# A lap in front of TensorE's loop that only branches through its program, in a decode attention kernel

## The chip, the cores and the metric

One core of a Trainium2 chip runs the whole kernel. The metric is device time in microseconds (us) of one execution, as the median of several runs. The core's engines are TensorE (PE in the profile, its weight loads PEld), VectorE (DVE), ScalarE (ACT), GpSimd (POOL) and SyncE (SP); each runs its own program, and they meet at semaphores. Sixteen DMA engines move data between main memory and the core's buffers.

## The reference

Attention for one new token: 32 query heads of 128 numbers, 8 heads of keys and values with 65,536 rows each, so that 4 query heads share one head of keys and values. Everything is bfloat16.

```
B, Hq, Hkv, Sq, Sk, D = 1, 32, 8, 1, 65536, 128
k = jnp.repeat(k, rep, axis=1)
v = jnp.repeat(v, rep, axis=1)
scale = D ** -0.5
scores = jnp.einsum("bhqd,bhkd->bhqk", q, k) * scale
p = _softmax(scores, axis=-1)
return jnp.einsum("bhqk,bhkd->bhqd", p, v)
```

Keys and values together are 268 MB, and each number of them is used for four query heads only.

## The kernel before

The work is cut into 16 pairs of units, two pairs to each of the 8 heads. A unit is 16,384 rows of keys and as many of values, laid out as 128 partitions with 128 rows each; `T` is 128, and the unit is handled in `G` = 16 groups of `TB` = 8 tiles of 128 x 128. A pair has 8.39 MB of keys and 8.39 MB of values.

TensorE's program (`tensor_engine`, L177) first transposes the queries (L180), which need a small DMA, and then runs a loop of 16 laps (`Fori`, L182), one for each pair. Its body, `pe_pair` (L164), is written out in full:

- for both units, group by group, eight transposes of key tiles into one of four PSUM buffers `trb` (`pe_transposes`, L131), and three groups behind (`LAG`) the eight score matmuls of an earlier group (`pe_scores`, L140);
- then for both units 128 matmuls that sum the values, weighted, in `pvb` (`pe_values`, L158). In the last lap only, one more matmul (L151) stands in the second unit's sum behind an `If` (L149).

So a lap has 768 matmuls, each with a weight load, and about 50 semaphore instructions. VectorE and ScalarE copy the transposed groups to the buffer `ktb` (`evict`, L189 to L201: VectorE three of four, ScalarE the fourth), find the maximum (L219), compute the exponentials (L336) and keep the sums.

SyncE issues all large DMAs, in the order keys of pair 0, values of pair 0, keys of pair 1, values of pair 1, and so on (L402 to L435). Pair 0's keys come as four transfers of 2 MB (L396) and its values as two of 4 MB (L428). The keys of pairs 1 to 13 come as one transfer of 8 MB into `kbuf` (L408); its second half is copied to `bbuf` by GpSimd and ScalarE (`copy_unit`, L203). There is one set of buffers for keys and one for values, so two waits order these issues: keys of the next pair wait for `kfree`, which comes when the last group of the first unit has been taken out of `trb` (L197), and for `cfree`; values of the next pair wait for `vfree`, which VectorE gives when the second unit's values have been summed (L284, L296). While TensorE works on keys, the queue holds the values, and the other way round.

ScalarE's part of the copies, two pieces in each of those laps, is made in `act_pair` behind the evictions of the groups 3 and 7. `own` (L118) lets an engine wait for its own instruction, and `copy_unit` calls it for the last of its pieces.

## Time and profile before

| | |
|---|---|
| runs (3) | median 628.36 us, 628.25 to 628.51 |
| the profiled execution | 628.33 us |
| its span, first to last instruction | 627.0 us |
| TensorE's mean granted clock | 0.773 |
| busy: PE, DVE, ACT, POOL | 489.3, 315.3, 231.7, 159.9 us |
| moved | 268.57 MB, mean 428 GB/s |
| packets of queue q8, kind instruction | 6, 0.10 MB |

The profile is of one execution. Its page has the busy share of every engine in 40 slices, the DMA queues, the chain of work that ended last, and groups of instructions; the views of the trace that are quoted below list instructions in order of time, or the waits, or the busy time by stretches. Times in them are microseconds from the first instruction. "Issue" as a releaser means that an engine stood still and the profile shows nothing that it waited for; "PEq" is the sequencer of TensorE, which takes the semaphores.

### The profile page before, as it was taken

The page shows a single profiled execution, that of the slowest core. Times are in us where ns is not written, and L with a number is a line of the kernel's source. Part 1 is how long each engine was busy: PE and PEld are TensorE (multiplying, and loading weights), DVE is VectorE, ACT ScalarE, POOL GpSimd, SP SyncE. Part 2 cuts the span into 40 slices and gives each one's busy share as a digit, 9 for nine tenths or more (in the row PEclk, how much of TensorE's full clock was granted, in tenths as well). Part 3 has the DMA queues.
Part 4 walks back from the last instruction along what each step waited for, and adds up shares of the span by engine and source line. Part 5 has one row for each costly group of instructions (what it writes and reads, how often), then busy time and mean ns, then how long its engine had stood idle before and what let it go on. Part 6 is the DMA issues. An engine that isn't in the chain of part 4 may idle for free. (4 is left out here: it accounts for less than half of the span.)

```text
span 627.0 us, 27922 instructions
## 1 busy us (share of the span) xinstructions
PE 489.3 (78%) x12292; PEld 482.7 (77%) x12292; DVE 315.3 (50%) x699; ACT 231.7 (37%) x445; POOL 159.9 (26%) x124
## 2 busy tenths in 40 slices
PE   4843995949859598694976949779596895999996
PEld 4842995949859598694977949679596895989896
DVE  4630653717537174471744718346183561848482
ACT  1320542515435153341634407244062441624241
POOL 0000704307042070520606115060250702400000
PEclk9875886959769597795977959669596885969696
DMA  8999999999999999999999999999999999999997
GB/s 368 433 454 424 439 431 439 431 439 431 439 422 447 414 452 414 452 414 440 431 426 439 431 439 431 439 431 439 431 439 431 439 431 435 418 429 431 418 431 316
DMA packets 6768, 268.57 MB, mean 428 GB/s; under 512 B 1000, under 2 KB 1128, under 8 KB 1256
## 3 DMA queue, kind: packets, MB, share of 16 engines
q1 hardware_dynamic: 6712, 268.45, 99.3%
q8 instruction: 6, 0.10, 0.1%
q10 hardware_dynamic: 48, 0.01, 0.0%
q14 instruction: 2, 0.02, 0.0%
HBM read 268.44 MB, written 0.01 MB: 428 GB/s over the span
## 5 line engine op out<-in xcount | busy, mean ns | idle before, releaser
L201 DVE COPY ktb<-trb 128x1024 bf16<-128x1024 bf16 x384 | 254.9, 689 | 169.1 <-PE trb L131 165.1
L199 ACT ACTIVATE ktb<-trb 128x1024 bf16<-128x1024 bf16 x128 | 131.0, 1023 | 341.1 <-PE trb L131 287.6
L131 PE MATMUL trb<-ident,kbuf 128*128 128x128 bf16 x2048 | 180.6, 247 | 94.9 <-PEq L46 94.8
L131 PEld LDWEIGHTS trb<-ident,kbuf 128*128 128x128 bf16 x2048 | 146.1, 112 | 95.8 <-issue 95.6
L207 POOL COPY bbuf<-kbuf 128x2048 bf16<-128x2048 bf16 x78 | 143.9, 1893 | 174.8 <-POOLq L46 174.8
L140 PE MATMUL qkb<-qcur,ktb 128*128 128x4 bf16 x4096 | 176.8, 165 | 9.2 <-PEq L46 7.3
L140 PEld LDWEIGHTS qkb<-qcur,ktb 128*128 128x128 bf16 x4096 | 158.2, 97 | 15.3 <-issue 15.0
L131 PE MATMUL trb<-ident,bbuf 128*128 128x128 bf16 x2048 | 156.9, 219 | 3.6 <-issue 3.6
L158 PE MATMUL pvb<-pts,vbuf 128*128 128x4 bf16 x4096 | 113.3, 166 | 23.2 <-PEq L46 12.8
L158 PEld LDWEIGHTS pvb<-pts,vbuf 128*128 128x128 bf16 x4096 | 111.3, 103 | 25.0 <-issue 24.1
L131 PEld LDWEIGHTS trb<-ident,bbuf 128*128 128x128 bf16 x2048 | 117.3, 97 | 1.1 <-issue 1.1
L382 POOL PARTITION_ALL_REDUCE cmaxa<-cmax x32 | 11.9, 370 | 252.3 <-POOLq L46 252.3
L336 ACT ACTIVATE pts<-qkb,negm 128x128 bf16<-128x128 f32 x128 | 50.5, 546 | 0.0
L345 ACT ACTIVATE bbuf<-kbuf 128x2048 bf16<-128x2048 bf16 x26 | 49.5, 1902 | 0.0
L336 ACT ACTIVATION_READ_ACCUMULATOR pts<-qkb,negm 128x1 f32 x128 | 35.4, 277 | 0.0
L219 DVE TENSOR_REDUCE cmax<-qkb 128x4 f32<-128x512 f32 x32 | 22.0, 686 | 19.3 <-DVEq L46 19.3
L332 ACT ACTIVATE alpha<-dm 128x4 f32<-128x4 f32 x32 | 6.4, 201 | 43.5 <-ACTq L46 43.5
L247 DVE TENSOR_TENSOR acc<-acc,pvb 128x4 f32<-128x4 f32 x16 | 2.5, 158 | 34.5 <-PE pvb L158 34.5
L384 POOL PARTITION_ALL_REDUCE la<-lp x8 | 3.4, 430 | 33.1 <-POOLq L46 33.1
L245 DVE COPY acc<-pvb 128x4 f32<-128x4 f32 x8 | 1.3, 163 | 17.8 <-PE pvb L158 17.8
L229 DVE TENSOR_TENSOR m<-m,cmaxa 128x4 f32<-128x4 f32 x24 | 3.9, 164 | 11.7 <-DVEq L46 11.5
L238 DVE TENSOR_TENSOR acc<-acc,alpha 128x4 f32<-128x4 f32 x24 | 3.9, 163 | 11.3 <-DVEq L46 11.3
(42 smaller groups left out, 39.1 us busy)
## 6 DMA issues: line engine op xcount, KB each, us to landing
vbuf<-in_v_dram SPq DMA_DIRECT2D x5, 4096.0 KB, 25.7
kbuf<-in_k_dram SPq DMA_DIRECT2D x4, 2048.0 KB, 15.5
bbuf<-in_k_dram SPq DMA_DIRECT2D x4, 2048.0 KB, 20.2
kbuf<-in_k_dram SPq DMA_DIRECT2D x1, 4096.0 KB, 16.3
bbuf<-in_k_dram SPq DMA_DIRECT2D x1, 4096.0 KB, 16.0
vbuf<-in_v_dram SPq DMA_DIRECT2D x1, 2336.0 KB, 29.0
vbuf<-in_v_dram SPq DMA_DIRECT2D x1, 1216.0 KB, 31.5
vbuf<-in_v_dram SPq DMA_DIRECT2D x1, 416.0 KB, 32.0
```

What stands on the lines that cost most here:

```text
L131: ins = pe.transpose(trb[j % NTB][:, i * P:(i + 1) * P], kv[:, t, :], ident[:, :])
L140: ins = pe.matmul(qkb[n][:, t * R:(t + 1) * R], lhsT=ktb[:, off:off + P], rhs=qcur[:, :], start=True, stop=True)
L158: ins = pe.matmul(pvb[n][:, 0:R], lhsT=vv[:, t, :], rhs=pts[n][:, t * R:(t + 1) * R], start=t == 0, stop=t == T - 1)
L199: e.activation(dst, trb[j % NTB][:, :], AF.Copy).then_inc(eva, 1)
L201: e.tensor_copy(dst, trb[j % NTB][:, :]).then_inc(evd, 1)
L207: ins = op(bbuf[:, c * CB * D:(c + 1) * CB * D], kbuf[:, off:off + CB * D])
L219: e.tensor_reduce(cmax[:, :], qkb[n][:, :].rearrange("p (t g) -> p g t", g=R), AX.X, ALU.max).then_inc(cm, 1)
L229: own(e, e.tensor_tensor(mn[:, :], mo[:, :], cmaxa[:, :], ALU.max), xd)
L332: e.activation(alpha[:, :], dm[:, :], AF.Exp, scale=scale)
L336: ins = e.activation(pv[:, g, :], sv[:, g, :], AF.Exp, bias=negm[:, g:g + 1], scale=scale, accum_out=rsum[:, g:g + 1])
L345: return e.activation(o, i, AF.Copy)
L382: e.partition_all_reduce(cmaxa[:, :], cmax[:, :], P, bass.bass_isa.ReduceOp.max).then_inc(cma, 1)
```

## The change

TensorE's loop has 17 laps in place of 16. The steps of `pe_pair` are first put in a list, with the values cut into steps of eight tiles, which makes 96 steps. The list is cut into sections of 14 steps (252 // 18), seven in all, and each is put behind a branch of its own, `If(lap > 0)`. In the first lap all seven branches are taken past their sections, and nothing else is done. At the end of the body, behind another branch (`If(lap == 0)`), stand the wait for the queries, their transpose and the wait for the float identity, which stood ahead of the loop. The `If` of the last lap compares with `NP` now in place of `NP - 1`. The matmuls, their order and their semaphores are those of before.

In `copy_unit`, an engine that gives no semaphore of its own doesn't wait for its copy; the copy itself raises the semaphore that TensorE waits for. ScalarE's first piece (behind group 3) uses this; the second piece still waits.

```
+SECTION = 252
...
-    def pe_values(pe, n, lap):
+    def pe_values(pe, n, t0, lap):
         vv = vbuf[:, n * T * D:(n + 1) * T * D].rearrange("p (t d) -> p t d", d=D)
-        for t in range(T):
+        for t in range(t0, t0 + TB):
             if n and t == V_PIECES[1][0]:
-                with pe.If(lap == NP - 1):
+                with pe.If(lap == NP):
...
-        ins.then_inc(pvd, 1)
+        if t == T - 1:
+            ins.then_inc(pvd, 1)
 
     def pe_pair(pe, lap):
-        pend = []
+        steps, pend = [], []
         for n in range(2):
             for j in range(G):
-                pe_transposes(pe, n, j)
+                steps.append((pe_transposes, n, j))
                 pend.append((n, j))
                 if len(pend) > LAG:
-                    pe_scores(pe, *pend.pop(0))
-        while pend:
-            pe_scores(pe, *pend.pop(0))
-        for n in range(2):
-            pe_values(pe, n, lap)
+                    steps.append((pe_scores, *pend.pop(0)))
+        steps += [(pe_scores, *x) for x in pend]
+        steps += [(pe_values, n, t, lap) for n in range(2) for t in range(0, T, TB)]
+
+        per = SECTION // (2 * TB + 2)
+        for i in range(0, len(steps), per):
+            with pe.If(lap > 0):
+                for f, *x in steps[i:i + per]:
+                    f(pe, *x)
 
     def tensor_engine(pe):
-        pe.wait_ge(q_sem, 16)
-        pe.wait_ge(t_id, 1)
-        pe.transpose(qps[:, 0:HR], qsb[:, :], ident[0:HR, 0:HR]).then_inc(s_x, 1)
-        pe.wait_ge(t_if, 1)
-        with pe.Fori(0, NP) as lap:
+
+        with pe.Fori(0, NP + 1) as lap:
             pe_pair(pe, lap)
+            with pe.If(lap == 0):
+                pe.wait_ge(q_sem, 16)
+                pe.wait_ge(t_id, 1)
+                pe.transpose(qps[:, 0:HR], qsb[:, :], ident[0:HR, 0:HR]).then_inc(s_x, 1)
+                pe.wait_ge(t_if, 1)
...
-                if c != copies[-1]:
+                if c != copies[-1] or not x:
                     ins.then_inc(done, 1)
-            own(e, ins, x)
-            e.sem_inc(done, 1)
+            if x:
+                own(e, ins, x)
+                e.sem_inc(done, 1)
...
-                copy_unit(e, (lap - (WHOLE[0] - 1)) * (WHOLE[1] - lap) > 0, ACT_COPIES[j], copy, cpa, xa)
+                copy_unit(e, (lap - (WHOLE[0] - 1)) * (WHOLE[1] - lap) > 0, ACT_COPIES[j], copy, cpa, xa if j == max(ACT_COPIES) else None)
```

## The prediction

> **What bounds the kernel now.** I read the page first: the slices, the queues, the chain that ended last.

> ```profile
> DMA  8999999999999999999999999999999999999997
> GB/s 368 433 454 424 439 431 439 431 439 431 439 422 447 414 452 414 452 414 440 431 426 439 431 439 431 439 431 439 431 439 431 439 431 435 418 429 431 418 431 316
> ...
> q1 hardware_dynamic: 6712, 268.45, 99.3%
> q8 instruction: 6, 0.10, 0.1%
> ...
> DMA 5%; PE 1%; SPq 0%; DVE 0%; issue 0%; DVEq 0%
> ...
> L131 PE MATMUL trb<-ident,kbuf 128*128 128x128 bf16 x2048 | 180.6, 247 | 94.9 <-PEq L46 94.8
> ```

> DMA is at 9 tenths in every slice but the first and the last, and the chain that ended last is DMA. The kernel is bound by moving 268.45 MB; no slice in between shows a hole to close. TensorE waits 94.9 us for keys, about 6.3 us in each of 15 laps. So the edit can cost time only by making a transfer start after its queue ran dry, and can gain hardly anything in the middle. Whether a transfer starts late depends on the first lap, so I read stretches of it (busy time by engine, granted clock, DMA share, GB/s) and SyncE's issues.

> ```profile
> 1.00:2.00 1.00, 0.00 (x0) 0.00 (x0) 0.52 (x3) 0.84 (x1) 0.38 (x1) 1.00 0.80 180
> 0.00:40.00 40.00, 27.50 (x582) 26.90 (x583) 20.65 (x53) 11.45 (x20) 1.46 (x8) 0.93 0.96 406
> 43.00:60.00 17.00, 5.51 (x187) 5.28 (x186) 0.81 (x5) 0.00 (x0) 0.00 (x0) 0.50 1.01 435
> ```

> ```profile
> 0.72 0.88 SPq L396 DMA_DIRECT2D kbuf<-in_k_dram  x2
> 1.65 1.14 SPq L396 DMA_DIRECT2D bbuf<-in_k_dram  x2
> 2.97 0.86 SPq L428 DMA_DIRECT2D vbuf<-in_v_dram  x2
> 21.01 0.33 SPq L408 DMA_DIRECT2D kbuf<-in_k_dram  x1
> 55.99 0.33 SPq L431 DMA_DIRECT2D vbuf<-in_v_dram  x1
> ```

> And how long the transfers of L428 (pair 0's values, two) and of L408 (pair 1's keys) took to land, from the queries of these two lines:

> ```profile
> DMA to landing us min/median/max: 30.7/35.4/40.1
> ...
> DMA to landing us min/median/max: 41.8/41.8/41.8
> ```

> Pair 0's keys and values are 16.78 MB. 40 us at 406 GB/s are 16.24 MB, the rest at 435 takes 1.2 us: on the mean the queue would be dry at 41.2 us, on the slowest engine near 43.4 (3.3 + 40.1, the landing). Pair 1's keys were issued at 21.0, far ahead. They are 8.39 MB, 19.3 us: dry again at 60.5 on the mean, and landed at 62.8 (21.0 + 41.8). Pair 1's values were issued at 55.99. From issue to data takes about 0.9 us (issue at 0.72; 0.42 us worth of traffic before 2.0, so a start near 1.6). **The slack is thus 18 to 21 us for pair 1's keys, and 3.6 to 5.9 us for its values.** These two bounds decide the case.

> **What the first lap pays for its program.** Next, TensorE's timeline of that lap.

> ```profile
> 8.29 3.57 PE L131 MATMUL trb<-ident,kbuf 128*128 128x128 bf16 x32 [2.95 <-PEq L46]
> ...
> 14.77 0.61 PE L131 MATMUL trb<-ident,kbuf 128*128 128x128 bf16 x8
> ...
> 20.18 0.21 PE L140 MATMUL qkb<-qcur,ktb 128*128 128x4 bf16 x3 [0.17 <-issue]
> ...
> 27.94 0.26 PE L131 MATMUL trb<-ident,bbuf 128*128 128x128 bf16 x1 [2.61 <-issue]
> ...
> 35.21 0.56 PE L131 MATMUL trb<-ident,bbuf 128*128 128x128 bf16 x7 [0.95 <-issue]
> ...
> 46.41 3.53 PE L158 MATMUL pvb<-pts,vbuf 128*128 128x4 bf16 x127 [6.33 <-issue]
> 53.61 0.28 PE L158 MATMUL pvb<-pts,vbuf 128*128 128x4 bf16 x5 [3.68 <-issue]
> ...
> 62.98 0.37 PE L131 MATMUL trb<-ident,kbuf 128*128 128x128 bf16 x2 [7.21 <-PEq L46]
> ```

> Five stops stand in the midst of a tile, with no releaser ("issue"), and none recurs in later laps. Between the stops at 46.41 and 53.61 lie 127 matmuls: with their weight loads and two semaphore instructions 256 instructions. Six instruction packets make 0.10 MB, 16 KB each; 256 instructions of 64 bytes fill one. So a stop is the arrival of a program block, and after the first lap the loop stays loaded. Stops that add up to 13.7 us (0.17 + 2.61 + 0.95 + 6.33 + 3.68) delay TensorE in lap 0, but the last values of pair 0 still end early enough: 55.99 lies 3.6 us or more ahead of need. **What the edit removes is off the path.**

> [...]

> **The price of the lap in front.** It cannot hide behind tiles, since it has none. Each section is under 256 instructions, so every branch lands in the same block or the next, and blocks are asked for one after another. Counting back 256 instructions from the stop at 20.18 leads to the eighth group's transposes at 14.77: that block was entered there, and the next was usable at 20.18, so 5.4 us from one entry to the next while 2 MB transfers fill the queues. Later ones took 7.8 (20.18 to 27.94), 7.3 (to 35.21), 11.2 (to 46.41) and 7.2 (to 53.61). Two blocks were there at the start (nothing stops before 20.18); the seven sections end in the seventh block, so five arrivals are walked through.

> Engines begin at 0.7 us; the loop's start and a taken branch bring 1.0. Four arrivals fall before 24 us, at 5.4: 22.6. The fifth meets the larger transfers, at 7.4 (between the 7.8 and 7.3 above): **30.0 us for the walk's end.** No row shows an arrival with the queues empty. Were each as quick as a data issue, 0.9 us, the walk would end at 5.5; with five at 7.4 it would end at 38.0. I stay near the five measured arrivals, since the data queues are full from 1.6 us on.

> Lap 1's end is SyncE's next issue of values:

> ```profile
> 95.19 0.33 SPq L431 DMA_DIRECT2D vbuf<-in_v_dram  x1
> ```

> Then come the transpose of the queries, the loop's branch and the wait for keys long landed: 0.5 us, so the first transposes at 30.5 in place of 8.29. The queries need no term: scores come more than 3 us behind the first transposes.
> - Keys of pair 1: 8.29 to 21.01 is 12.7, so issue at 43.2, data at 44.1. The queue is dry from 41.2 to 43.4: a hole of 0.7 to 2.9 us.
> - Values of pair 1: lap 0 without its stops took 55.99 − 8.29 − 13.7 = 34.0 to the issue; lap 1 took 32.2 (62.98 to the issue at 95.19). I take 33.0, and 0.5 for seven branches: issue at 64.0, data at 64.9. Needed were 60.5 (mean) to 62.8 (slowest): 2.1 to 4.4 us late. The second hole contains the first; the larger total counts.

> The loop's branch, and TensorE's last rows:

> ```profile
> L182 PEldq COMPARE_BRANCH  x16: 67/208/219, 55.3 to 625.0; - x16
> ```

> ```profile
> 623.33 1.68 PE L158 MATMUL pvb<-pts,vbuf 128*128 128x4 bf16 x55 [0.21 <-DMA vbuf<-in_v_dram]
> ```

> Since the end waits for whole landings, that is for the slowest engine, I take 2.6, near the lower of the two. The lost DMA time isn't regained, as later slices are full.

> Small parts: a branch not taken costs 0.067 us, taken 0.208 (least and median of the loop's branch, L182). Seven not taken and one taken are 0.7 us in each lap, covered by the 6.3 us wait for keys; without that cover 16 laps would pay 11 us. In the last lap some four lie behind the last keys, 0.3 us, against 0.21 us in which TensorE waits for values at 623.33: 0.1 us. ScalarE's first copy no longer waits for itself; ScalarE is busy 37% and that wait ends nothing on the path: 0. The same blocks are fetched in either kernel, so DMA carries no more.

> Sum, against the profiled execution's own 628.33 us (median of the runs 628.36): 628.33 + 2.6 + 0.1 = **631.0 us**.

> **The rivals.**
> 1. The walk ends by about 27.5 us, and both transfers still start in time: 628.4 us. For it: 28.0 with five arrivals at 5.4 lies next to that point, and one row alone gives the 5.4. It decides where an arrival takes under 5.3 us on average. Against: the fifth arrival meets the value transfers. This ends not slower. Chance 0.30.
> 2. The walk is slow throughout, all five arrivals at 7.4 or more: a walk to 38.0 and more, the values' data at 72.9, 10.1 us later than 62.8: 638.4. For it: four of five measured arrivals; against: none of these fell under 2 MB transfers. Chance 0.09.
> 3. The walked blocks don't stay. Then lap 0 stalls again, 13.7 us more behind the walk: 2.6 + 13.7, 644.7 us. Against: six packets in 16 laps. [...] Chance 0.02.
> 4. Faster: the slowest engine lies 2.3 us behind the mean at 62.8 against 60.5, and instruction packets in the midst of data may be part of why. If the walk fetched before the queues fill, up to that much could come back: 626.1. Against: the queues fill at 1.6 us, and the walk's second arrival is behind that. Chance 0.03.

> **How the numbers follow.** My case, a walk of 28 to 36 us, has 0.56; it gives 0.5 to 8 us more. A measurement of this kernel can tell about 0.2% (1.26 us) from no change. Slower by over that: 0.56 + 0.09 + 0.02 = 0.67; faster 0.03; within 0.30. The range holds rival 1 and my case up to a walk of 35 us (7.1 us late, 635.5): 628.0 to 635.5 us. Outside stay rivals 2, 3 and 4 and the top of my case, under 2 in 10. The likeliest case's own range is 628.9 to 635.5.

> **What would show each step.** Right: TensorE's first transposes of keys at about 30 us, not 8.3; its first lap then without "issue" stops of over 0.2 us; six or so instruction packets, all but one before 31 us; pair 1's keys issued near 43 and its values near 64; slices 3 to 5 of GB/s lower; later laps as before, with waits for keys shorter by 0.7 us. Wrong: a walk that ends before 27 us, with GB/s full; instruction packets in each lap; or pair 1's values issued late for another reason, such as a longer first lap.

## The result, and the profile after

The changed kernel takes 632.26 us (median of 6 runs, 631.71 to 633.23) against 628.47 us (6 runs, 628.25 to 628.71). The ratio is 1.0061, with a 95% interval of 1.0048 to 1.0074: 3.8 us slower. The profiled execution took 632.37 us with a span of 630.7 us.

The page of the changed kernel, with the same parts as before:

```profile
DMA  8989999999999999999999999999999999999997
GB/s 363 430 344 462 403 466 399 466 399 466 399 466 399 466 399 466 399 466 400 465 411 453 424 441 428 436 441 424 449 416 457 407 457 407 430 432 432 416 445 306
...
q1 hardware_dynamic: 6712, 268.45, 98.8%
q8 instruction: 6, 0.10, 0.1%
...
L133 PE MATMUL trb<-ident,kbuf 128*128 128x128 bf16 x2048 | 177.7, 245 | 92.5 <-PEq L48 92.5
...
L191 PE MATMUL pvb<-ident,qsb 32*128 32x32 bf16 x1 | 0.2, 181 | 30.8 <-issue 30.8
```

The third slice has fallen to 344 GB/s, and it is the only one with a hole; the slices behind it alternate more than before, but their mean is nearly the old one (399 and 466 make 432.5, 439 and 431 made 435). The instruction packets are six, as before. TensorE's first work of any kind, the transpose of the queries, now stands behind 30.8 us in which nothing ran there. The branches of the lap in front, of which L180 is the line, tell what filled them; the row covers the stretch from the start to 31.3 us:

```profile
L180 PEldq COMPARE_BRANCH  x7: 219/5659/6005, 1.0 to 24.7; - x7
```

The seven branches took (ns, in order) 358, 5659, 6005, 219, 5320, 5687 and 5880. Read by these times, five led to a block that was not there, the fourth stayed in its block, and the first led to one that was loaded at the start. From 31.5 us on, 112 such branches have a median of 65 ns. TensorE's start and SyncE's issues:

```profile
30.83 0.18 PE L191 MATMUL pvb<-ident,qsb 32*128 32x32 bf16 x1 [30.83 <-issue]
31.82 0.48 PE L133 MATMUL trb<-ident,kbuf 128*128 128x128 bf16 x3 [0.81 <-PEq L48]
```

```profile
43.63 0.33 SPq L418 DMA_DIRECT2D kbuf<-in_k_dram  x1
63.48 0.33 SPq L441 DMA_DIRECT2D vbuf<-in_v_dram  x1
```

And the hole itself, in stretches of 2 us, with three stretches around the values' issue:

```profile
40.00:42.00 2.00, 2.00 (x53) 2.00 (x51) 1.40 (x3) 1.02 (x1) 0.00 (x0) 1.00 0.84 360
42.00:44.00 2.00, 2.00 (x54) 2.00 (x52) 1.60 (x3) 0.33 (x1) 0.00 (x0) 1.00 0.00 0
44.00:46.00 2.00, 2.00 (x55) 2.00 (x53) 1.84 (x3) 0.70 (x1) 0.00 (x0) 1.00 1.52 524
...
60.00:62.00 2.00, 2.00 (x82) 2.00 (x78) 0.32 (x2) 0.00 (x0) 0.00 (x0) 0.50 0.53 229
62.00:64.00 2.00, 1.26 (x48) 1.17 (x44) 0.16 (x1) 0.00 (x0) 0.00 (x0) 0.50 1.22 524
64.00:66.00 2.00, 0.00 (x0) 0.00 (x0) 0.00 (x0) 0.00 (x0) 0.00 (x0) 0.50 1.47 524
```

DMA share is 0.00 from 42 to 44 us while TensorE is fully busy: the keys' buffer isn't free yet, and pair 1's keys are issued at 43.63. A packet counts with its whole time in the stretch in which it begins, so a share can exceed 1. The 0.00 means that no data packet began; those begun earlier ended by 43.2 us, and the first of the keys began at 44.6. Around the values' issue there is no hole: the three shares have a mean of 1.07.

Packet by packet, the trace tells more. From 100 to 600 us 16.0 packets are in flight on the mean, as many as there are DMA engines, so I count each one fewer than 16 as an idle engine. Counted so, the engines stood idle for 2.8 us on the mean between 36 and 50 us, and for 0.03 between 50 and 75.

The waits of TensorE, summed, show the other side of the edit:

```profile
PE trb L133 <- PEq L48: 92.5, 16, 7.8
PE pvb L191 <- issue: 30.8, 1, 30.8
PE pvb L160 <- PEq L48: 13.5, 17, 2.1
```

The stops "issue" at transposes and values, 3.6 and 10.2 us before, are gone. Lap 0 runs without a stop.

### The profile page after: what moved, and what is told of

It is laid out like the page before. It is cut to its first block, busy times and chain, and to the rows that moved or that the text cites. A ratio compares the mean times of both kernels' runs of the same rounds, so it can differ in the third digit from the quotient of the medians.

```text
span 630.7 us, 28036 instructions
## 1 busy us (share of the span) xinstructions
PE 483.8 (77%) x12292; PEld 478.3 (76%) x12292; DVE 314.8 (50%) x699; ACT 231.3 (37%) x445; POOL 160.1 (25%) x124
## 3 DMA queue, kind: packets, MB, share of 16 engines
q1 hardware_dynamic: 6712, 268.45, 98.8%
## 5 line engine op out<-in xcount | busy, mean ns | idle before, releaser
L133 PE MATMUL trb<-ident,kbuf 128*128 128x128 bf16 x2048 | 177.7, 245 | 92.5 <-PEq L48 92.5
L133 PEld LDWEIGHTS trb<-ident,kbuf 128*128 128x128 bf16 x2048 | 144.2, 111 | 93.4 <-issue 93.4
L142 PEld LDWEIGHTS qkb<-qcur,ktb 128*128 128x128 bf16 x4096 | 156.8, 97 | 11.1 <-issue 10.6
L133 PE MATMUL trb<-ident,bbuf 128*128 128x128 bf16 x2048 | 155.3, 218 | 0.0
L160 PE MATMUL pvb<-pts,vbuf 128*128 128x4 bf16 x4096 | 113.0, 166 | 13.7 <-PEq L48 13.5
L346 ACT ACTIVATION_READ_ACCUMULATOR pts<-qkb,negm 128x1 f32 x128 | 35.4, 276 | 0.0
L191 PE MATMUL pvb<-ident,qsb 32*128 32x32 bf16 x1 | 0.2, 181 | 30.8 <-issue 30.8
L191 PEld LDWEIGHTS pvb<-ident,qsb 32*128 32x128 bf16 x1 | 0.1, 98 | 30.8 <-issue 30.8
L342 ACT ACTIVATE alpha<-dm 128x4 f32<-128x4 f32 x32 | 6.4, 201 | 43.4 <-ACTq L48 43.4
L257 DVE TENSOR_TENSOR acc<-acc,pvb 128x4 f32<-128x4 f32 x16 | 2.5, 158 | 30.8 <-PE pvb L160 30.8
(42 smaller groups left out, 47.7 us busy)
```

What stands on the lines that cost most here:

```text
L133: ins = pe.transpose(trb[j % NTB][:, i * P:(i + 1) * P], kv[:, t, :], ident[:, :])
L142: ins = pe.matmul(qkb[n][:, t * R:(t + 1) * R], lhsT=ktb[:, off:off + P], rhs=qcur[:, :], start=True, stop=True)
L160: ins = pe.matmul(pvb[n][:, 0:R], lhsT=vv[:, t, :], rhs=pts[n][:, t * R:(t + 1) * R], start=t == 0, stop=t == T - 1)
L342: e.activation(alpha[:, :], dm[:, :], AF.Exp, scale=scale)
L346: ins = e.activation(pv[:, g, :], sv[:, g, :], AF.Exp, bias=negm[:, g:g + 1], scale=scale, accum_out=rsum[:, g:g + 1])
```

## The experiments

The theory: the whole loss comes from TensorE starting its first lap late, since SyncE's issues of pair 1's keys and values then come behind the point at which the queues run dry. The rivals put the loss on the branches in every lap, or on the walk or a lap in front as such. A second question is what makes one block's arrival 5.7 us long.

**The changed kernel without the lap in front.**

```
-        with pe.Fori(0, NP + 1) as lap:
+        with pe.Fori(1, NP + 1) as lap:
             pe_pair(pe, lap)
```
with the queries' transpose ahead of the loop again, as in the kernel before.

> The changed kernel without its lap in front: the seven branches stand in each of 16 laps, the queries are transposed ahead of the loop as before. Theory (the late start of TensorE's first lap is all of the cost): first transposes at 8.3 us, the five stops of lap 0 back, pair 1's values issued near 56, time 628.5 us, at most 0.3 above before. Rival (the branches themselves cost some 0.24 us in each of 16 laps): 632 us.

Measured: 628.54 us against 628.42, ratio 1.0002 (0.9993 to 1.0011). First transposes at 8.09 us, the stops back, values issued at 53.32. But the seven branches aren't in the program that ran: its trace has no row for L180, where the changed kernel has 119 branches, presumably because `lap > 0` always holds in a loop that starts at 1. So this run says nothing of the rival of the branches. It shows that ScalarE's copy without a wait, which this kernel has too, costs 0.1 us, which is within the noise. The branches are tested below, in the kernel whose walk precedes all transfers.

**The kernel before, started late.**

```
         pe.wait_ge(t_if, 1)
+        pe.wait_ge(kp[1][1], 16)
         with pe.Fori(0, NP) as lap:
```

> The kernel before, with one wait more ahead of the loop: TensorE starts only when pair 0's last key piece has landed (24.0 us). No branch and no walk. Theory (late start): first transposes at 24.2, pair 1's keys issued at 37 to 39, so no or nearly no hole there; lap 0 keeps its stops and lasts 47.7 us, pair 1's values issued near 72, 10 to 12 us behind need, time 638 to 640 us. Rival (walk or branches cost by themselves, start is not decisive): 628.5 us.

Measured: 635.41 us, ratio 1.0114 (1.0099 to 1.013), 7.0 us slower with neither branch nor walk. SyncE's issues, and three stretches around the second:

```profile
36.06 0.33 SPq L409 DMA_DIRECT2D kbuf<-in_k_dram  x1
66.62 0.33 SPq L432 DMA_DIRECT2D vbuf<-in_v_dram  x1
```

```profile
60.00:62.00 2.00, 1.11 (x41) 1.11 (x42) 0.00 (x0) 0.00 (x0) 0.00 (x0) 0.50 0.00 0
62.00:64.00 2.00, 2.00 (x81) 2.00 (x79) 0.65 (x4) 0.00 (x0) 0.00 (x0) 0.50 0.03 8
64.00:66.00 2.00, 1.88 (x68) 1.79 (x66) 0.00 (x0) 0.00 (x0) 0.00 (x0) 0.50 0.03 8
```

Keys in time, no hole at 42; values late, and no packet began from 60 to 66 us, but for the two last blocks of the program (0.03). Packets begun earlier ended by 62.4, and the values' first began at 67.6. The theory holds, though 638 to 640 us were expected: the lap, from the first transposes at 23.27 to the values' issue, took 43.4 us in place of 47.7, 3.1 of it by shorter stops (10.6 us in place of 13.7).

**The changed kernel, held a little more.**

```
                 pe.wait_ge(t_if, 1)
+                pe.wait_ge(vp[0][0], 16)
```

> The changed kernel, held further: at the end of the lap in front TensorE also waits for the first half of pair 0's values (lands at 34.0 us). Theory: first transposes at 35.0 in place of 31.8, the hole ahead of pair 1's keys grows by as much, time 632.3 + 3.2 = 635.5 us, a slope of one. Rival (the start does not decide): 632.3 us.

```profile
47.00 0.33 SPq L419 DMA_DIRECT2D kbuf<-in_k_dram  x1
66.85 0.33 SPq L442 DMA_DIRECT2D vbuf<-in_v_dram  x1
```

Measured: 636.44 us (635.64 to 637.22), ratio 1.0132 (1.0117 to 1.0148). In the profiled execution, of 635.64 us, the first transposes came at 35.24 us, 3.4 later than in the changed kernel, and both issues were 3.4 later; the time is 3.3 longer (the medians are 4.2 apart). The slope of one is there. The hold itself did little of it: in this execution the walk took to 33.4 us, with arrivals of up to 6.6 us. The same walk thus took 30.6 us in one execution and 33.4 in another; a walk that varies would fit the changed kernel's wider spread, 1.5 us against 0.5.

**Fewer arrivals: sections of 28 steps.** `SECTION = 504`, four branches.

> The changed kernel with sections of 28 steps: four branches in place of seven, the third of which leads over one block of the program. Theory: the walk has four arrivals in place of five and ends at 25 us, first transposes at 26, pair 1's keys issued at 38, before the queue is dry; if the block that is jumped is absent, lap 0 has one stop of 4 to 7 us, and pair 1's values are issued at 58 (no stop) or 62 to 65 (stop): 628.5 to 632 us, one hole or none, and none ahead of the keys. Rival (cost by branches): 4/7 of 3.8 us, 630.6, with the keys' hole as it is.

```profile
39.43 0.33 SPq L418 DMA_DIRECT2D kbuf<-in_k_dram  x1
59.29 0.33 SPq L441 DMA_DIRECT2D vbuf<-in_v_dram  x1
```

Measured: 630.08 us (629.56 to 631.57), ratio 1.003 (1.0019 to 1.0041). The walk ended at 25.9 us; lap 0 had no stop, so the block that was jumped had arrived as well: the third branch took 7.6 us, and two instruction packets came during it. More than half of the loss is gone with one arrival less. The rival's 630.6 us is near, but it kept the keys' hole, and the keys were issued in time here. What is left, 1.7 us, is more than the two issues tell; pair 1's keys landed at 63.8 (39.4 + 24.4) against 62.8, so the slowest engine was 1.0 us late. The rest stays open.

**One branch over the whole body.** `SECTION = 1728`.

> The changed kernel with a single section: one branch over the whole body. Theory (only arrivals that are walked cost): the lap in front fetches the block of its target alone and ends near 7 us, before the first keys land; lap 0 starts at 8.3 and stops at the blocks in between as before, pair 1's keys are issued by 22 and its values by 57; time 628.5 us. Rival (a lap in front costs by itself, or a far branch loses the first blocks and more): keys issued after 40 or values after 59.6, over 630 us.

```profile
9.76 3.57 PE L133 MATMUL trb<-ident,kbuf 128*128 128x128 bf16 x32 [2.86 <-PEq L48]
```

```profile
21.65 0.33 SPq L418 DMA_DIRECT2D kbuf<-in_k_dram  x1
55.96 0.33 SPq L441 DMA_DIRECT2D vbuf<-in_v_dram  x1
```

Measured: 628.65 us against 628.39, ratio 1.0004 (0.9994 to 1.0013). The branch took 5.4 us, one arrival; the stops of lap 0 are back (13.2 us of "issue"), and the time is that of before. A lap in front costs next to nothing by itself (0.3 us). Instruction packets were eight in place of six.

**The walk ahead of all transfers.**

```
                 pe.wait_ge(t_if, 1)
+                pe.sem_inc(walked, 1)
...
+        e.wait_ge(walked, 1)
         for p in range(NP):
```
The second wait is SyncE's, ahead of its first key transfer.

> The changed kernel, with SyncE's first key transfer held until the lap in front has ended, so that five arrivals are walked with empty data queues. Theory (an arrival waits behind data packets): arrivals of 2.5 to 4 us in place of 5.5 to 6, the walk ends at 13 to 21 us, all transfers start that much later, and lap 0 then has no hole: 628.5 + 13 to 21 = 641 to 649 us. Rival (an arrival has a fixed latency of 5.7 us): walk ends at 30, 658 us.

```profile
L181 PEldq COMPARE_BRANCH  x7: 219/2967/3334, 1.0 to 14.4; - x7
```

```profile
17.78 1.73 SPq L408 DMA_DIRECT2D kbuf<-in_k_dram  x2
...
37.23 0.33 SPq L421 DMA_DIRECT2D kbuf<-in_k_dram  x1
64.13 0.33 SPq L444 DMA_DIRECT2D vbuf<-in_v_dram  x1
```

Measured: 645.43 us (2 runs), 17.0 us above 628.39. With no data transfers in the queues an arrival takes 2.9 to 3.3 us, so about half of the 5.7 us is the data traffic. The first issue moved from 0.72 to 17.78, 17.1 us, and the time by 17.0. This kernel has all seven branches in each lap, at 65 to 77 ns when not taken, so the rival of the branches, with its 3.8 us, is out. In this kernel lap 0 has no stop and no transfer is late: so taking the 13.7 us of stops away is worth nothing, even where the walk makes no hole.

**Smaller data packets.** Pair 0's keys as 16 transfers of 0.5 MB, with the counts of the semaphores raised to match.

> The changed kernel with pair 0's keys as 16 transfers of 0.5 MB in place of four of 2 MB, so that the packets that an instruction packet meets up to 22 us are 4 KB in place of 16 KB. Theory (an arrival waits for one to three data packets of its engine): arrivals of 4 to 5.2 us, the walk ends at 23 to 28, pair 1's keys issued at 36 to 41, 628.5 to 630 us. Rival (the wait does not depend on packet size): arrivals of 5.5 to 6, walk to 30, 632.3 us.

```profile
L181 PEldq COMPARE_BRANCH  x7: 219/5280/6045, 1.0 to 23.7; - x7
```

Measured: 632.37 us against 628.39, ratio 1.0059 (1.0043 to 1.0076). The five arrivals took 4.7 to 6.0 us with packets a quarter as large, against 5.3 to 6.0 in the changed kernel, and the walk ended at 29.5 against 30.6. So my notion of a wait behind one to three packets falls. What in the traffic adds the 2.5 us or so isn't settled; an amount of data in flight that does not depend on the packets' size would fit, and wasn't tried. The time of this kernel says little on the start, since it moved less up to 40 us: 393 GB/s, against 404 in the changed kernel.

The two bounds of the prediction, taken on the mean over the engines, are an issue of pair 1's keys by 40.3 us (41.2 less 0.9) and of its values by 59.6 (60.5 less 0.9). Against them, in profiled executions:

| kernel | keys' issue | values' issue | late by (larger of the two) | engines idle longer | packets took longer | time above before |
|---|---|---|---|---|---|---|
| changed | 43.63 | 63.48 | 3.9 | 2.7 | 1.1 | 3.9 (632.37 − 628.47) |
| before, started late | 36.06 | 66.62 | 7.0 | 6.1 | 0.6 | 6.6 (635.01 − 628.42) |
| changed, held | 47.00 | 66.85 | 7.3 | 5.9 | 1.2 | 7.2 (635.64 − 628.42) |
| sections of 28 steps | 39.43 | 59.29 | 0 | 0.5 | 0.5 | 1.3 (629.75 − 628.42) |
| one section | 21.65 | 55.96 | 0 | 0.1 | 0.1 | 0.4 (628.81 − 628.39) |
| without the lap in front | 20.07 | 53.32 | 0 | −0.1 | 0.1 | 0.1 (628.50 − 628.42) |
| small packets | 42.41 | 62.17 | 2.6 | 1.6 | 2.9 | 4.2 (632.63 − 628.39) |

Idle time and packet time are means over the 16 engines for the whole execution, less those of the kernel before (5.6 and 622.4 us); together they give the time to 0.3 us. The idle time is the loss that the theory names. In the kernel that started late it lies ahead of the values; in the changed kernel and the held one it lies ahead of the keys, and next to nothing ahead of the values (0.03 us in either): where the keys come late, the values are needed later too. So the lateness of the values agrees with the time of these two kernels without being its cause. Behind a hole, the packets of pair 1's transfers also took longer, 0.6 to 1.2 us in sum; why stays open.

No kernel here beats the one before, and the reason is its first view: its queues have no hole in the middle, so there is nothing for TensorE's first lap to give back.

## Why the prediction was right

The sign and the mechanism, a late start that makes an issue late and a queue dry, were right, and 632.26 us lies between 628.0 and 635.5; the likeliest value was 631.0. Which of the two issues makes the hole was wrong: it is the keys', not the values'. By its steps:

- **What the edit removes is off the path.** Right: the kernel whose walk precedes the transfers has no stops and is longer by its later start alone (17.0 against 17.1 us).
- **The walk's end, 30.0 us.** Measured 30.6 (30.8 for the queries' transpose). Two errors in it cancelled: arrivals under the 2 MB transfers took 5.3 to 6.0 us, not 5.4, and the fifth took 5.9, not 7.4. The longer intervals of lap 0, 7.2 and more, were no measure of an arrival in the walk.
- **Keys' issue 43.2, values' issue 64.0.** Measured 43.63 and 63.48. The first transposes came at 31.82, 1.3 us later than forecast, since the way from the walk's end to them takes 1.2 us and not 0.5; from there to the keys' issue it was 11.8 us in place of 12.7, and to the values' issue 31.7 in place of 33.5.
- **The term that was mis-sized: 2.6 us for the hole.** The time rose by 3.8. I had 2.1 us for the slowest engine and 4.4 for the mean, both for late values, and chose near the lower; with the measured issue at 63.48 these would be 1.6 and 3.9. The trace has no such hole. The engines stood idle ahead of pair 1's keys, 2.8 us on the mean, which lies in the 0.7 to 2.9 that I had for that hole and set aside. The other 1.1 us is packets that took longer, a term that I put at nothing. So it was luck that 2.6 came near the idle time, and luck that 3.9 agrees with the measured time.
- **Slack of pair 1's keys, 18 to 21 us.** By the prediction's own numbers it is 19.3 to 21.5; nothing hangs on it.
- **Branches and ScalarE's copy, 0.1 us.** Right within the uncertainty: the copy cost 0.1 us in the kernel without the lap in front, within the noise, and the kernel whose walk precedes the transfers has both and is longer by its later start alone. A branch not taken measured 65 to 77 ns, as priced.
- **Later waits for keys shorter by 0.7 us.** Not so: from 75 us on they sum to 88.8 us, against 84.6 before. TensorE was busy for less time as well (483.8 us against 489.3, at a granted clock of 0.788 against 0.773), so the branches can't be read from these waits.
- **The rivals.** A walk of 38 us didn't come, the longest seen was 33.4. The walk that ends by 27.5 us and costs nothing isn't borne out either: with sections of 28 steps it ended at 25.9 us and still cost 1.7. That blocks don't stay is out: six packets again, five of them before 31 us, and no stop in lap 0. In lap 0 of the kernel before, with matmuls between them, five crossings stopped TensorE for 13.7 us (0.17 to 6.33 each); in the walk, where taken branches led to them, five blocks took 5.3 to 6.0 us each.
- **Slices 3 to 5 lower.** Only slice 3 is; slices 4 and 5 have a mean of 432.5 GB/s (462 and 403), against 431.5 before (424 and 439), as there is no second hole.

## What to carry to other kernels

A stall that nothing waits for isn't worth removing: find first which issue the stalled engine releases, and how long before its queue runs dry. The walk through TensorE's program was a serial chain of arrivals (five, one after another, 5.3 to 6.0 us each in the changed kernel). Taken ahead of all transfers it cost its full length (17.0 us); in the first pass of the kernel before, the work between the arrivals hid part of them (13.7 us of stops, against 28.6 us for the five of the changed kernel's walk). For an engine that only frees buffers, one date matters, the latest issue that keeps the queue from running dry; behind it, 3.4 us more of delay cost 3.3 here. And where a run is to test an instruction, look first whether its trace has that instruction.
